# Order of code, branch hints, two moved steps and sums of h in PSUM in an attention, routing and expert kernel

## The chip, the cores and the metric

The kernel runs on one core of a Trainium2 chip. The metric is device time in microseconds (us) of one execution. The core has five engines that run their own instruction streams and meet through semaphores: TensorE (PE, matrix products into PSUM; its weight loads are listed as PEld), VectorE (DVE), ScalarE (ACT), GpSimd (POOL) and SyncE (SP, which here issues most DMAs). A suffix q (PEq, ACTq) marks what an engine's sequencer does: branches, semaphores, register work, DMA issues. The granted clock is the share of full speed that the throttle gave TensorE.

## The reference

Three stages: attention with a window and sink tokens, routing of every token to one of 8 experts, and the expert's two-layer network.

```python
B, H, S, D = 4, 8, 768, 64          # n_sink 4, window 128 (inputs)
scores = matmul(q, k.T) / sqrt(D)
keep = (pos_k < n_sink) | ((0 <= rel) & (rel < window))
x = matmul(softmax(where(keep, scores, -1e9)), v)      # -> [B, S, 512]
...
logits = x @ w_gate                  # 8 experts
local = sigmoid(x @ w_local)
e = argmax(logits) if s == 0 or local < 0.5 else the expert of token s - 1
p = softmax(logits)
out = p[e] * (relu(x @ w1[e]) @ w2[e])     # w1: 512 x 1024, w2: 1024 x 512
```

All inputs are fp32. The kernel gets the products' accuracy by splitting a number into a high part (rounded to fp32r) and a low part (the rest): x w = xh wh + xl wh + xh wl. So each matrix has a "high" tile, made by a cast, and a "low" tile, made by a subtraction.

## The kernel before

**Attention, twice.** `attention(fast)` is traced twice under one runtime `If` (L985): once for a narrow window with few sinks (`narrow != 0`, what these inputs take), once as the general code (`Else`). Both are instructions in one program, the fast code in front and the general code behind it. All five engines meet the branch at the start; at the end of the fast code they branch over the general code to the join, where the rest of the program begins.

**Early expert steps.** While the fast attention runs out, the first expert's first 256 tokens ("early") go through the first layer. There are FC = 8 steps f, one for each 128 of the 1024 hidden columns. `early_first(f, hs)` (its matmuls are L449, its activation L453, its subtraction L454) makes one: 12 matmuls into the PSUM tile `hs`, relu on ScalarE for the high part, and on VectorE max(h, 0) minus the high part for the low part. The matmuls and the activation are issued at the call; the subtraction is the function it returns, called later (`low_steps`). In the fast code the order of TensorE, ScalarE, VectorE and SP is written out by hand, so each engine runs its instructions as the code lists them. The tail of that list is `first_steps(5)`, `low_steps(2)`, `first_steps(6, 7)`, `low_steps(4)`.

**Behind the join** (L1232 on, also in an order by hand): SP issues three loads of weights; ScalarE casts the second layer's weights w2 of the first expert to their high part in 8 instructions (`second_high`, L1226), VectorE makes the low parts in 8 subtractions; then TensorE multiplies the early tokens' relu(h) with w2 high (`late_product`, L1229, 32 matmuls). SP fetches the next rows of x from DRAM, where the attention and the routing have scattered them (`xrsn`, L1054), TensorE transposes them (L425), and the products with w2 low follow. ScalarE, VectorE and POOL also prepare the weights of the coming expert: a cast (L1028) and a subtraction (L1029, part of them on POOL).

**Experts.** For each of the 8 experts a `Switch` chooses one of 25 arms by the number of token groups left. Its dispatch branches stand in the profile at L1421, its hints at L1264 and, as the first instruction of an arm, L1295. In an arm, `ffn1` runs the first layer over a group of ng units of 32 tokens (n = 32 ng columns), again in 8 steps f. For ng <= MERGE = 7 a step accumulates two halves side by side into one PSUM tile `hp` of [128, 2, n] (L1111), VectorE adds the two halves (L1114, a reduction) into an SBUF tile `hs`, ScalarE takes relu of `hs` (L1131) and VectorE the low part (`low`, L1099, which reads `hs` and the high part in `hq`). For larger groups the PSUM tile itself is `hs` (L1120). `ps_h` has three buffers. Between the steps, transposes of the next rows of x (L425) with a cast (L428), a subtraction (L431) and copies of metadata (L427) are put in, and after them come the second layer's products (L1169), the scaling by the gate (L1150) and the scatter to the output (L1151, a DMA issued by POOL).

Of the kernel before, what the change touches and what calls it, by code (L numbers as in the profile page):

```python
# [9 lines left out]
F32 = mybir.dt.float32  # L10
# [7 lines left out]
ET = mybir.EngineType  # L18

P = 128  # L20
HT = 32
# [7 lines left out]
KC = DM // P  # L29
FC = FF // P  # L30
# [12 lines left out]
NE = 2  # L43
MERGE = 7
LIMIT = 24
WARM = 12
STEPS = {2: 1, 3: 2, 4: 1, 5: 1, 9: 1, 10: 1, 11: 2}
ENDING = {38: 1, 39: 2, 40: 1, 41: 1, 42: 1, 43: 1, 44: 2, 45: 1, 46: 2}
# [20 lines left out]
def kernel(ctx, tc, qkd, vn, vs, w1, w2, nw, c_misc, c_ident, c_idw, c_small,  # L69
# [3 lines left out]

    const = ctx.enter_context(tc.tile_pool(name="const", bufs=1))
    dram = ctx.enter_context(tc.tile_pool(name="dram", bufs=1, space=bass.MemoryType.DRAM))

    x_a = const.tile([P, KC * 2 * GMAX * P], F32R, name="x_a")
    xm_a = [const.tile([P, GMAX + 1, 2], I32, name=f"xm{t}") for t in range(2)]
# [136 lines left out]
    with tc.issue_after(flag_op.ins) if FLAGF else ExitStack():  # L215
        for f in lead0[0:2]:
            f()

    narrow = nc.values_load(flag_i[0:1, 0:1], min_val=0, max_val=1,
                            skip_runtime_bounds_check_because="a product of comparisons")  # L220
# [222 lines left out]
    n_e = NE * P  # L443
# [67 lines left out]
    def attention(fast):  # L511
        sfx = "f" if fast else "g"
        with ExitStack() as st:
# [227 lines left out]
            if fast:  # L741
# [62 lines left out]
                for n in range(nb):  # L804
                    now, a, z, y = (blocks[x] if 0 <= x < nb else [] for x in (n, n - 1, n - 2, n - 3))
                    nm = f"{sfx}{n}"
# [54 lines left out]
                nm = f"{sfx}{nb}"  # L861
# [12 lines left out]
                def first_steps(*fs):  # L874
                    for f in fs:
                        if f in (4, 5):
                            pl, tag, w = ((ps_a, "a", n_e), (ps_b, "b", 512))[f - 4]
                            hs = pl.tile([P, w], F32, tag=tag, name=f"he{sfx}{f}")[:, 0:n_e]
                        else:
                            if f % 2 == 0:  # L880
                                first_ps.append(ps_s.tile([P, 2, 512], F32, tag="s", name=f"he{sfx}{f}"))
                            hs = first_ps[-1][:, f % 2, 0:n_e]
                        lows_f.append(early_first(f, hs))
# [3 lines left out]
                def low_steps(k):  # L887
                    for _ in range(k):
                        lows_f.pop(0)()
# [53 lines left out]
                next(tail_r, None)  # L943
                masked()
                first_steps(5)
                low_steps(2)
                first_steps(6, 7)
                low_steps(4)
                order.close()
            else:  # L950
# [28 lines left out]
                    low()  # L979
                counts(ps_m, m_tag)  # L980
                masked()
                for f in range(FC):
                    early_first(f, ps_s.tile([P, 2, 512], F32, tag="s", name=f"he{sfx}{f}")[:, 0, 0:n_e])()

    with tc.If(narrow != 0) as branch:  # L985
        attention(True)
    with branch.Else():
        attention(False)
# [6 lines left out]
    s_p = ctx.enter_context(tc.tile_pool(name="sp", bufs=2))  # L995
    ps_h = ctx.enter_context(tc.tile_pool(name="ps_h", bufs=3, space=PS))
# [12 lines left out]
    def w_load(i, behind=None):  # L1009
        e, c = divmod(i, NCH)  # L1010
        if e >= E:
            return
        t = raw_t[i % AHEAD]
        if c < KC:
            d = nc.sync.dma_start(t, w1[e, c * P:(c + 1) * P, :])
            if behind is not None:
                tc.add_manual_dep(d.ins, behind.ins.name, mybir.DependencyInfo(
                    mybir.DependencyClass.Sync, mybir.DependencyReason.DATA), reason="behind the jumps")
        else:
            w2_load(t, e, c - KC)  # L1020
# [70 lines left out]
    def ffn1(e, xt, ng, nm, ag):  # L1091
        xx, meta = xt
        h1, l1 = w1_of(e)
        n = ng * HT
        held = []

        def low(cuts):
            for d, h in cuts:
                nc.vector.scalar_tensor_tensor(out=d[:, :, 1, :], in0=h, scalar=0.0,  # L1099
                                               in1=d.bitcast(F32)[:, :, 0, :], op0=ALU.max, op1=ALU.subtract)  # L1100

        for f in range(FC):
            fs = slice(f * P, (f + 1) * P)
            if ng <= MERGE:
                hp = ps_h.tile([P, 2, n], F32, tag="h", name=f"h{nm}_{f}")
                m = 2 if ng <= 4 else 1
                mm = [x for k in range(KC) for x in ((hp, h1[:, k, fs], xx[:, k, :, :n]),
                                                     (hp[:, 0:m, :], l1[:, k, fs], xx[:, k, 0:m, :n]))]
                mm[-2:] = mm[:-3:-1]
                for t, (o, w, x) in enumerate(mm):  # L1110
                    nc.tensor.matmul(o, w, x, start=t == 0, stop=t == len(mm) - 1, skip_group_check=True)  # L1111
                hs = s_p.tile([P, MERGE * HT], F32, tag="hs", name=f"hs{nm}_{f}")
                hs = hs[:, :n]
                nc.vector.tensor_reduce(out=hs, in_=hp.rearrange("p a n -> p n a"), axis=AX.X, op=ALU.add)  # L1114
            else:
                hs = ps_h.tile([P, GMAX * P], F32, tag="h", name=f"h{nm}_{f}")
                hs = hs[:, :n]
                mm = [(w, xx[:, k, a, :n], k) for k in range(KC) for w, a in ((h1, 0), (h1, 1), (l1, 0))]
                for t, (w, x, k) in enumerate(mm):
                    nc.tensor.matmul(hs, w[:, k, fs], x, start=t == 0, stop=t == len(mm) - 1)  # L1120
            rest, nf = n % P, n // P * P
            cuts = []
            if rest:
                r = hx[:, f, 2 * nf:2 * nf + 2 * (rest if nf else P)]
                cuts.append((r.rearrange("p (j a c) -> p j a c", j=1, a=2)[:, :, :, 0:rest],
                             hs[:, nf:n].rearrange("p (j c) -> p j c", j=1)))
            if nf:
                cuts.append((hx[:, f, 0:2 * nf].rearrange("p (j a c) -> p j a c", a=2, c=P),
                             hs[:, 0:nf].rearrange("p (j c) -> p j c", c=P)))
            for d, h in cuts:  # L1130
                relu = nc.scalar.activation(d[:, :, 0, :], h, AF.Relu)  # L1131
            if f == 0:
                ag.begun = relu
            if ng > MERGE:
                low(cuts)
            else:
                low(held)
                held = cuts
            ag.run(time1(ng) / FC)
        low(held)  # L1140
# [81 lines left out]
    h2, l2 = w2_of(0)  # L1222

    def second_high(raw, h):
        for s in halves:
            nc.scalar.copy(h[:, s], raw[:, s])  # L1226
# [5 lines left out]
    with tc.manual_schedule(engines=set(ORDERED)):  # L1232
        for c in range(3):
            w_load(NCH + c)
        for c in range(KC):
            h, l = h2(2 * c, 2), l2(2 * c, 2)
            second_high(second_raw[c], h)
            for s in halves:
                last_low = nc.vector.tensor_tensor(out=l[:, s], in0=second_raw[c][:, s], in1=h.bitcast(F32)[:, s],
                                                   op=ALU.subtract)  # L1240
        for f in range(FC):
            for j in (1, 0):
                for a in range(2):
                    late_product(f, j, a, h2, start=f + a == 0)
# [21 lines left out]
    for c in range(2):  # L1266
        h, l = [t[:, c, :] for t in w1_of(1)]
# [157 lines left out]
```

## Time and profile before

| | us |
|---|---|
| median of 3 runs | 578.47 |
| lowest, highest run | 575.3, 579.16 |
| the profiled execution, device time | 580.11 |
| its span, first to last instruction | 578.3 |
| TensorE busy | 526.2 (91%) |
| mean granted clock | 0.954 |

The profile shows one execution. Busy times are sums of the instructions' times on an engine; matmuls are pipelined, so their ends are modelled. A timeline lists an engine's instructions in order of start, with equal neighbours put together (x24 is 24 of them) and in brackets the idle time before them and the instruction that ended it. A line of a group gives the shortest, median and longest duration in ns, the first and last start in us, and the shapes. A row of a window gives its length, then each engine's busy time, the granted clock, the share of time in which the DMA engines were busy, and GB/s.

In 40 equal slices of 14.5 us the busy tenths of TensorE, and the granted clock, are:

```profile
PE   6699989979997989787999999899999799999994
PEclk8599989899998989989899999999999899999999
```

### The profile page before, as it was taken

What the parts mean: (1) busy time and instruction counts of PE and PEld (TensorE: products, weight loads), DVE (VectorE), ACT (ScalarE), POOL (GpSimd) and SP (SyncE); (2) the same over time, 40 slices, a digit from 0 to 9 for tenths busy, and PEclk for the clock granted to TensorE, in tenths of its full rate; (3) what the DMA queues carried; (4) which work ended last, traced back from release to release, by engine and by line L of the source; (5) the groups of instructions that cost most, each with busy time, mean ns of one, the idle gap of its engine ahead of it and who ended that gap; (6) DMA issues with size and microseconds to landing.
All of it is one profiled execution on the core that took longest, in us unless ns stands there. A gap on an engine that the chain in (4) does not pass through costs nothing. (4 is left out here: it accounts for less than half of the span.)

```text
span 578.3 us, 11794 instructions
## 1 busy us (share of the span) xinstructions
PE 526.2 (91%) x3933; PEld 451.0 (78%) x3933; DVE 343.4 (59%) x1270; ACT 285.0 (49%) x854; POOL 228.2 (39%) x191
## 2 busy tenths in 40 slices
PE   6699989979997989787999999899999799999994
PEld 3588878868886879676889697889888489889893
DVE  4587777687777777647256274653474937363321
ACT  3588868667766785253253080633432635024120
POOL 3963625475265073334260062443502635204101
PEclk8599989899998989989899999999999899999999
DMA  8624404170436025374571274747514656111000
GB/s 300 234 117 177 155 22 176 38 238 32 154 112 201 2 111 183 132 224 141 184 247 39 78 272 112 262 134 239 205 40 141 239 170 245 55 30 50 19 23 35
DMA packets 30474, 80.53 MB, mean 139 GB/s; under 512 B 3646, under 2 KB 5310, under 8 KB 30272
## 3 DMA queue, kind: packets, MB, share of 16 engines
q1 hardware_dynamic: 25520, 65.41, 33.3%
q0 software_dynamic: 4176, 12.64, 5.8%
q14 instruction: 148, 1.21, 0.7%
q8 instruction: 54, 0.88, 0.6%
q10 hardware_dynamic: 576, 0.39, 0.2%
HBM read 63.41 MB, written 16.06 MB: 137 GB/s over the span
## 5 line engine op out<-in xcount | busy, mean ns | idle before, releaser
L619 ACT ACTIVATE pef<-smf,biasf 128x264 f32<-128x264 f32 (+2 forms) x192 | 93.6, 489 | 42.9 <-DVE biasf L616 42.7
L1131 ACT ACTIVATE hq<-h 128x256 fp32r<-128x256 f32 (+3 forms) x72 | 24.2, 360 | 110.4 <-PE h L1120 94.7
L616 DVE CUSTOM_DVE_ANT_0 smf<-sf,mask 128x264 f32<-128x264 f32 (+2 forms) x192 | 66.6, 402 | 10.3 <-PE sf L604 9.7
L1169 PE MATMUL late<-w_a,hq 128*128 128x512 f32 (+2 forms) x288 | 70.2, 398 | 1.2 <-issue 1.2
L1099 DVE SCALAR_TENSOR_TENSOR hq<-h,hq 128x256 fp32r<-128x256 f32 (+3 forms) x72 | 26.6, 390 | 68.6 <-ACT hq L1131 67.1
L1169 PEld LDWEIGHTS late<-w_a,hq 128*128 128x128 f32 (+2 forms) x288 | 50.8, 179 | 15.8 <-issue 1.7
L1151 POOL DMA_INDIRECT out_dram<-ot_d,oi_d x18 | 18.7, 1036 | 94.0 <-DVE ot_d L1150 74.3
L634 PE MATMUL tpf<-ident,pef 128*128 128x128 f32 x352 | 55.2, 302 | 0.2
L641 ACT COPY ptf<-tpf 128x512 f32<-128x512 f32 (+1 forms) x96 | 50.9, 531 | 1.6 <-PE tpf L634 1.6
L1131 ACT ACTIVATE hq<-hs 128x96 fp32r<-128x96 f32 (+2 forms) x72 | 16.7, 273 | 68.2 <-DVE hs L1114 61.0
L670 PE MATMUL avf<-ptf,v 128*64 128x128 f32 x704 | 50.2, 284 | 0.0
L634 PEld LDWEIGHTS tpf<-ident,pef 128*128 128x128 f32 x352 | 41.8, 152 | 7.8 <-issue 1.1
L1169 PE MATMUL late<-w_b,hq 128*128 128x512 f32 (+1 forms) x168 | 42.1, 409 | 0.8 <-ACT x_a L428 0.8
L670 PEld LDWEIGHTS avf<-ptf,v 128*64 128x64 f32 x704 | 38.5, 139 | 4.9 <-issue 0.3
L576 DVE TENSOR_TENSOR xb<-bkf,rsf 128x256 f32<-128x256 f32 x48 | 20.3, 423 | 32.8 <-ACT ptsf L651 31.2
L1169 PEld LDWEIGHTS late<-w_b,hq 128*128 128x128 f32 (+1 forms) x168 | 32.0, 192 | 9.5 <-ACT x_a L428 1.2
L1029 POOL TENSOR_TENSOR w_c<-raw,w_c 128x1024 fp32r<-128x1024 f32 x10 | 25.1, 2515 | 33.5 <-ACT w_c L1028 22.8
L1029 POOL TENSOR_TENSOR w_a<-raw,w_a 128x1024 fp32r<-128x1024 f32 x10 | 26.5, 2652 | 27.7 <-ACT w_a L1028 25.5
L604 PE MATMUL sf<-w_a 64*128 64x264 f32 (+2 forms) x288 | 28.2, 330 | 9.3 <-POOL w_a L134 6.5
L619 ACT ACTIVATION_READ_ACCUMULATOR pef<-smf,biasf 128x1 f32 x192 | 36.3, 189 | 0.0
L560 PE MATMUL bkf<-idw,xtf 128*128 128x146 f32 x192 | 34.7, 306 | 0.4
L1120 PEld LDWEIGHTS h<-x_a,w_c 128*128 128x128 f32 x288 | 34.3, 188 | 0.7 <-issue 0.6
(218 smaller groups left out, 1116.1 us busy)
## 6 DMA issues: line engine op xcount, KB each, us to landing
raw<-in_dram SPq DMA_DIRECT2D x53, 512.0 KB, 5.4
raw<-in_dram SPq DMA_DIRECT2D x14, 800.0 KB, 5.8
xr_0n<-xs SPq DMA_DIRECT2D x21, 258.0 KB, 4.2
v<-in_dram SPq DMA_DIRECT2D x7, 768.0 KB, 4.3
raw_w<-in_dram SPq DMA_DIRECT2D x7, 512.0 KB, 5.6
raw<-in_dram SPq DMA_DIRECT2D x10, 256.0 KB, 4.7
xs<-zrow SPq DMA_DIRECT2D x9, 258.0 KB, 5.5
xr_0r<-xs SPq DMA_DIRECT2D x8, 258.0 KB, 3.3
```

The lines of the kernel that those rows point to most:

```text
L560: mm = nc.tensor.matmul(bk[:, pr * WX:(pr + 1) * WX], blk["xt"][:, pr, :], idw[:, g * NPR + pr, :], start=True, stop=True, skip_group_chec ...
L604: u["mm"] = nc.tensor.matmul(sps[:, t, :w], qx[ROWS[t], i * P:(i + 1) * P], kx[ROWS[t], off:off + w], start=m == 0, stop=m == 2)
L616: u["dve"] = nc.vector.tensor_tensor_reduce(out=sm[:, :w], in0=sps[:, t, :w], in1=mk, scale=-0.125, scalar=BIG, op0=ALU.add, op1=ALU.min, ...
L619: nc.scalar.activation(pe[:, h, :w], sm[:, :w], AF.Exp, bias=bias[:, t:t + 1], scale=-1.0, accum_out=z[:, h, 0:1])
L634: nc.tensor.transpose(tp[:, t, k, :], pe[:, 2 * c + t, o:o + P], ident)
L641: nc.scalar.copy(pt[:, :, 0:nt, :], tp[:, :, 0:nt, :])
L670: nc.tensor.matmul(avt[ROWS[t], pr, :], prep["v"][:, j, 2 * pr + t, :], x["pt"][:, t, k, :], start=i < 2 and pr == 0 and k == 0, stop=pr = ...
L1029: todo += [lambda s=s: lo(out=l[:, s], in0=raw[:, s], in1=h.bitcast(F32)[:, s], op=ALU.subtract) for s in ([slice(0, FF)] if eng[1] == "po ...
L1099: nc.vector.scalar_tensor_tensor(out=d[:, :, 1, :], in0=h, scalar=0.0, in1=d.bitcast(F32)[:, :, 0, :], op0=ALU.max, op1=ALU.subtract)
L1120: nc.tensor.matmul(hs, w[:, k, fs], x, start=t == 0, stop=t == len(mm) - 1)
L1131: relu = nc.scalar.activation(d[:, :, 0, :], h, AF.Relu)
L1169: nc.tensor.matmul(o, a, w, start=t == 0, stop=t == len(mm) - 1, skip_group_check=half)
```

## The change

1. **Order of code.** `If` gets a label and `preferred_fallthrough_block=False`: the general code now stands in front and the fast code behind it. At the start every engine that takes the fast code branches over the general code; at the end of the fast code it goes on into the join without a jump. A hint with the branch's target ("LikelyTaken") is issued by each of the five engines as the first instruction of the kernel.
2. **Early steps.** `FIRST_F = 6`: the attention makes steps 0 to 5 only. Steps 6 and 7 move behind the join, into the block written out by hand, each with a PSUM tile of its own from `ps_h`. On ScalarE the order becomes: two casts of w2, the activation of step 6, two casts, the activation of step 7, four casts. On VectorE the two subtractions of steps 6 and 7 come first, then the eight of w2's low part.
3. **Sums of h.** Where 3n <= 512, that is for ng <= 5, the PSUM tile gets a third part of n columns, and the reduction writes the sum `hs` there and not into SBUF. The activation and the low part then read it from PSUM.

```diff
@@ -43,6 +43,7 @@
 NE = 2
 MERGE = 7
 LIMIT = 24
+FIRST_F = 6
 WARM = 12
 STEPS = {2: 1, 3: 2, 4: 1, 5: 1, 9: 1, 10: 1, 11: 2}
 ENDING = {38: 1, 39: 2, 40: 1, 41: 1, 42: 1, 43: 1, 44: 2, 45: 1, 46: 2}
@@ -73,6 +74,8 @@
 
     const = ctx.enter_context(tc.tile_pool(name="const", bufs=1))
     dram = ctx.enter_context(tc.tile_pool(name="dram", bufs=1, space=bass.MemoryType.DRAM))
+
+    tc.mark_branch_hint_location("mode", "LikelyTaken", engines=[ET.SP, ET.DVE, ET.PE, ET.Activation, ET.Pool])
 
     x_a = const.tile([P, KC * 2 * GMAX * P], F32R, name="x_a")
     xm_a = [const.tile([P, GMAX + 1, 2], I32, name=f"xm{t}") for t in range(2)]
@@ -943,8 +946,6 @@
                 next(tail_r, None)
                 masked()
                 first_steps(5)
-                low_steps(2)
-                first_steps(6, 7)
                 low_steps(4)
                 order.close()
             else:
@@ -979,10 +980,10 @@
                     low()
                 counts(ps_m, m_tag)
                 masked()
-                for f in range(FC):
+                for f in range(FIRST_F):
                     early_first(f, ps_s.tile([P, 2, 512], F32, tag="s", name=f"he{sfx}{f}")[:, 0, 0:n_e])()
 
-    with tc.If(narrow != 0) as branch:
+    with tc.If(narrow != 0, preferred_fallthrough_block=False, label="mode") as branch:
         attention(True)
     with branch.Else():
         attention(False)
@@ -1102,15 +1103,18 @@
         for f in range(FC):
             fs = slice(f * P, (f + 1) * P)
             if ng <= MERGE:
-                hp = ps_h.tile([P, 2, n], F32, tag="h", name=f"h{nm}_{f}")
+                hp3 = ps_h.tile([P, 3 if 3 * n <= 512 else 2, n], F32, tag="h", name=f"h{nm}_{f}")
+                hp = hp3[:, 0:2]
                 m = 2 if ng <= 4 else 1
                 mm = [x for k in range(KC) for x in ((hp, h1[:, k, fs], xx[:, k, :, :n]),
                                                      (hp[:, 0:m, :], l1[:, k, fs], xx[:, k, 0:m, :n]))]
                 mm[-2:] = mm[:-3:-1]
                 for t, (o, w, x) in enumerate(mm):
                     nc.tensor.matmul(o, w, x, start=t == 0, stop=t == len(mm) - 1, skip_group_check=True)
-                hs = s_p.tile([P, MERGE * HT], F32, tag="hs", name=f"hs{nm}_{f}")
-                hs = hs[:, :n]
+                if 3 * n <= 512:
+                    hs = hp3[:, 2]
+                else:
+                    hs = s_p.tile([P, MERGE * HT], F32, tag="hs", name=f"hs{nm}_{f}")[:, :n]
                 nc.vector.tensor_reduce(out=hs, in_=hp.rearrange("p a n -> p n a"), axis=AX.X, op=ALU.add)
             else:
                 hs = ps_h.tile([P, GMAX * P], F32, tag="h", name=f"h{nm}_{f}")
@@ -1232,9 +1236,18 @@
     with tc.manual_schedule(engines=set(ORDERED)):
         for c in range(3):
             w_load(NCH + c)
+        first_lows = []
         for c in range(KC):
             h, l = h2(2 * c, 2), l2(2 * c, 2)
             second_high(second_raw[c], h)
+            if FIRST_F + c < FC:
+                first_lows.append(early_first(FIRST_F + c, ps_h.tile([P, n_e], F32, tag="h", name=f"hl{c}")))
+            elif first_lows:
+                for f in first_lows:
+                    f()
+                first_lows = []
+        for c in range(KC):
+            h, l = h2(2 * c, 2), l2(2 * c, 2)
             for s in halves:
                 last_low = nc.vector.tensor_tensor(out=l[:, s], in0=second_raw[c][:, s], in1=h.bitcast(F32)[:, s],
                                                    op=ALU.subtract)
```

## The prediction

> **What bounds the kernel now.** I read the page first, then TensorE's timeline from the end of the attention on, then the windows of granted clock, and then, at every stop of TensorE, the timelines of the engine that it waited for.
>
> ```profile
> span 578.3 us, 11794 instructions
> PE 526.2 (91%) x3933; PEld 451.0 (78%) x3933; DVE 343.4 (59%) x1270; ACT 285.0 (49%) x854; POOL 228.2 (39%) x191
> ```
>
> TensorE is busy for 91% of the span. So time is won only where TensorE stands still or runs slowly, and work taken off another engine counts only if TensorE waits for it. The profiled execution took 580.11 us, 1.81 more than its span and 1.64 above the median of 578.47; I add my sum to the median. Its timeline (start, time taken, what; in brackets the idle time before it and who ended it):
>
> ```profile
> 237.90 3.04 PE L449 MATMUL hef<-x_a,w_a 128*128 128x256 f32 x24
> 241.42 1.68 PE L449 MATMUL hef<-x_a,w_a 128*128 128x256 f32 x12 [0.47 <-ACT hq L453]
> 247.40 9.26 PE L1229 MATMUL late<-w_b,hq 128*128 128x512 f32 x32 [4.30 <-ACT w_b L1226]
> 256.50 1.03 PE L425 MATMUL xpsn<-ident,xrsn 128*128 128x128 f32 x8
> 261.57 2.79 PE L1111 MATMUL h<-x_b,w_a 128*128 128x128 f32 x24
> 269.51 0.62 PE L425 MATMUL xp_0n<-ident,xr_0n 128*128 128x128 f32 x4
> 273.54 1.09 PE L425 MATMUL xp_0n<-ident,xr_0n 128*128 128x128 f32 x4 [3.41 <-issue]
> 275.47 7.49 PE L1169 MATMUL late<-w_b,hq 128*128 128x512 f32 x24 [0.84 <-ACT x_a L428]
> 453.88 1.09 PE L425 MATMUL xp_0n<-ident,xr_0n 128*128 128x128 f32 x4 [2.76 <-issue]
> ```
>
> Three stops stand out: 4.30 us where the attention ends (the join), 3.41 us in the first expert, 2.76 us in the sixth. Behind each the clock falls. In the windows (length, busy time of PE, PEld, DVE, ACT, POOL, granted clock) that follow a window with over 2 us of idle TensorE, it is 0.50:
>
> ```profile
> 244.97:248.39 3.42, 0.99 (x4) 0.86 (x5) 0.85 (x2) 1.73 (x4) 0.00 (x0) 1.00 0.33 90
> 248.39:251.80 3.41, 3.41 (x9) 2.65 (x8) 2.09 (x4) 3.41 (x7) 0.00 (x0) 0.50 0.82 216
> 251.80:255.20 3.40, 3.40 (x16) 2.73 (x15) 2.30 (x8) 1.20 (x3) 1.12 (x1) 1.00 0.87 262
> 272.28:275.70 3.42, 1.32 (x5) 0.98 (x6) 3.15 (x13) 1.31 (x3) 1.48 (x2) 0.50 0.37 103
> 275.70:279.11 3.41, 3.41 (x9) 2.64 (x10) 0.27 (x1) 0.00 (x0) 0.00 (x0) 0.50 0.89 286
> 453.19:456.60 3.41, 2.71 (x9) 1.70 (x10) 3.41 (x11) 3.41 (x10) 0.62 (x1) 0.50 0.88 326
> ```
>
> At 0.50 some 8 products of 512 columns begin in 3.41 us (0.427 us each), at full clock between 14 and 15 (0.235). A slow window full of work costs about 1.5 us.
>
> **The join, part by part.** The fast attention ends with the two last early steps (6 and 7); then the engines jump over the general attention's code.
>
> ```profile
> L985 PEldq COMPARE_BRANCH  x2: 83/2012/3942, 5.8 to 241.5; - x2
> 243.14 0.38 ACT L453 ACTIVATE hq<-hef 128x256 fp32r<-128x256 f32 x1 [1.77 <-PE hef L449]
> 246.66 4.26 ACT L1226 CAST w_b<-raw 128x512 fp32r<-128x512 f32 x8 [3.14 <-PEq L1258]
> 239.61 1.41 DVE L454 SCALAR_TENSOR_TENSOR hq<-hef,hq 128x256 fp32r<-128x256 f32 x4
> 246.31 1.86 SPq L1054 DMA_DIRECT2D xrsn<-xs  x3
> ```
>
> TensorE's branch at 241.5 takes 3.94 us against 0.08 at the kernel's start, where it falls through; ScalarE, done at 243.52, casts again at 246.66 (3.14 idle). Both are late by the same jump, so both must lose it, and with the fast code behind the general code both do. Removed: 4.30 idle, the 0.47 wait between steps 6 and 7 (one shared tile before, two now), and the slow window 1.5: 6.3 us.
>
> What is late next: TensorE may have to wait behind the join for the other engines' last work in the attention. Nothing before shows that wait. Its nearest row is VectorE's four sums for steps 2 to 5, which end at 241.02. Step 5 ends at about 239.42 (half of the 3.04 us for 24 matmuls from 237.90), so up to 1.6 us come back. Bounds: no wait, and one until 246.3, when SP fetches rows of x (behind the last scatter), which puts the products about where they stand. I take the 1.6: **4.7 us won** (0 to 6.3). The moved work itself (24 matmuls, 2 activations at 0.38, 2 of VectorE's sums) counts the same in both places, and issues no DMA. On ScalarE the activations now stand among the eight casts (4.26 us for all); a pair of casts takes 1.1 us while TensorE has 3.0 us of steps, so this is covered; without that cover TensorE would wait one pair, 1.1 us. VectorE's subtractions on w2 now follow the two sums, with all casts ahead of them. The rows of x are asked for at 246.31 to 248.17 and land 3.2 us later, by 251.4; TensorE, with 241.0 + 3.0 of steps + 32 products at 0.235, reaches them at 251.6. So they are just in time, and winning more than 4.9 us here would meet this load.
>
> ```profile
> xrsn<-xs SPq DMA_DIRECT2D x3, 258.0 KB, 3.2
> ```
>
> **The sums of h in PSUM.** The condition 3n <= 512 holds up to n = 160: by the reductions below (8 steps f a group) for three groups, one of 64 columns (first expert) and two of 160 (fifth, sixth).
>
> ```profile
> L1114 DVE TENSOR_REDUCE hs<-h x40: 275/492/626, 264.2 to 513.5; 128x224 f32<-128x448 f32 x16, 128x160 f32<-128x320 f32 x16, 128x64 f32<-128x128 f32 x8
> 268.09 4.66 POOL L1029 TENSOR_TENSOR w_c<-raw,w_c 128x1024 fp32r<-128x1024 f32 x2 [4.88 <-DMA raw_w<-in_dram]
> 268.34 2.20 DVE L1099 SCALAR_TENSOR_TENSOR hq<-hs,hq 128x64 fp32r<-128x64 f32 x1
> 270.85 1.99 DVE L1099 SCALAR_TENSOR_TENSOR hq<-hs,hq 128x64 fp32r<-128x64 f32 x1
> 272.76 0.68 DVE L431 TENSOR_TENSOR x_a<-xp_0n,x_a 128x512 fp32r<-128x512 f32 x1
> 449.67 2.37 POOL L1029 TENSOR_TENSOR w_c<-raw,w_c 128x1024 fp32r<-128x1024 f32 x1 [1.30 <-PE h L1111]
> 449.71 2.57 DVE L1099 SCALAR_TENSOR_TENSOR hq<-hs,hq 128x32 fp32r<-128x32 f32 x2
> L1099 DVE SCALAR_TENSOR_TENSOR hq<-hs,hq x72: 176/263/2373, 264.9 to 515.2; 128x128 fp32r<-128x128 f32 x32, 128x96 fp32r<-128x96 f32 x16, 128x32 fp32r<-128x32 f32 x16, 128x64 fp32r<-128x64 f32 x8
> L1099 DVE SCALAR_TENSOR_TENSOR hq<-h,hq x72: 179/418/557, 285.1 to 560.2; 128x256 fp32r<-128x256 f32 x48, 128x32 fp32r<-128x32 f32 x8, 128x96 fp32r<-128x96 f32 x8, 128x384 fp32r<-128x384 f32 x8
> ```
>
> The low part of relu(h) (L1099) reads hs and hq. With hs in SBUF it takes 0.18 us at best and up to 2.37: each long one lies under a POOL subtraction (L1029) and ends with it (268.34 + 2.20 = 270.54; POOL's first half ends at about 270.4). The same form that reads its first input from PSUM (hq<-h) never exceeds 0.56, for shapes up to twelve times as wide, and starts from the same 0.18 (for 32 columns): so I take the lock away and no change of the free duration. The trace has no reduction that writes PSUM; as its input is in PSUM already I put it at no change, 0 +/- 0.5 for the 24 steps (an estimate: 20 ns a step either way).
>
> First expert: TensorE stood for 3.41 us until VectorE, locked twice, came to L431 (272.76 to 273.44); two slow windows follow, with 1.32 and 3.41 us of matmuls at half speed, some 2.3 us lost. Removed 5.7.
>
> Sixth: 2.76 idle to 453.88, again behind a lock (2.57 us at 449.71), and 2.71 us at half speed, 1.2 lost (part of that window is idle). Removed 4.0. The fifth has no such stop.
>
> What is late next: a buffer of h comes free when hs has been read for the last time, by L1099, and no longer when the sum has been taken. There are three; step f+3 of TensorE needs the low part of f, which stands behind the sum of f+1 and behind ScalarE's activation, and that behind casts:
>
> ```profile
> 264.61 0.26 ACT L1131 ACTIVATE hq<-hs 128x64 fp32r<-128x64 f32 x1 [4.13 <-DVE hs L1114]
> 264.78 1.12 ACT L1028 CAST w_c<-raw 128x512 fp32r<-128x512 f32 x2
> 265.81 0.25 ACT L1131 ACTIVATE hq<-hs 128x64 fp32r<-128x64 f32 x1
> ```
>
> TensorE makes a step in 0.93 us (24 matmuls, three steps, in 2.79); ScalarE, with two casts (1.12 together) between the activations at 264.61 and 265.81, in 1.20. Over four steps with casts this runs 4 times 0.27, 1.1 us, behind. I charge it in the first and the sixth expert, and 0.4 in the fifth, whose pace I estimate as less tight. Residual stops, since the transposes wait for loads and VectorE's L431 anyway: 0.5 in the first, 0.9 in the sixth. **First expert: 5.7 - 1.1 - 0.5 = 4.1 won** (bounds -1.1, where only the later release acts, to 5.7); **sixth: 4.0 - 1.1 - 0.9 = 2.0** (-1.1 to 4.0); **fifth: -0.4** (0 to -1.0).
>
> **The order of code and the hints.** The general code now stands in front, so the jump that the join loses moves to the start, where all five engines go over it to the fast code. Instructions of hints themselves cost 0.05 us each. What would hide a late engine there:
>
> ```profile
> 14.78 1.62 POOL L129 CAST hq<-raw 128x800 fp32r<-128x800 f32 x2 [0.82 <-DMA raw<-in_dram]
> 21.52 0.81 PE L604 MATMUL sf<-w_a 64*128 64x264 f32 x4 [2.55 <-POOL w_a L134]
> L1264 ACTq BRANCH_PREFETCH_HINT  x1: 50/50/50, 247.5 to 247.5; - x1
> L1421 ACTq COMPARE_BRANCH  x16: 37/42/63, 260.1 to 559.9; - x16
> L1295 ACTq BRANCH_PREFETCH_HINT  x8: 36/40/40, 262.6 to 520.7; - x8
> ```
>
> TensorE waits 2.55 us for POOL at 21.52, and POOL for a load at 14.78. A jump of 3 us on TensorE, VectorE or ScalarE right behind its branch, TensorE's being at 5.8, lies ahead of these waits; only one on SP, which still has loads to ask for, delays them in full. Nearest rows for a jump with a hint: ScalarE's at the dispatch, hinted at 247.5, branches at 260.1 and begins its arm at 262.6, 2.5 us later. So: 0 (hidden, or the hint holds) to 2.5 (SP unhinted in effect). I take **-0.3**, since the hints are the first instructions, 5.8 us ahead of TensorE's branch (the L985 row), and all engines but SP have cover.
>
> [...]
>
> **Sum.** Join 4.7 + first expert 4.1 + sixth 2.0 - fifth 0.4 - start 0.3 = 10.1 us. The profiled execution would take 570.0, the median **568.4**.
>
> **The rivals.**
>
> *The PSUM sums win nothing.* POOL's subtraction then holds up VectorE's next operation with two inputs in SBUF (its own share of L1029), or the later release eats the gain. For it: TensorE waits for L431, not for L1099. Against it: 2.20 and 1.99 us are each an L1099. What is left is 4.7 - 0.4 - 0.3 = 4.0: 574.5.
>
> *The start pays the jump.* The hints come to nothing, as ScalarE's at the dispatch; SP's loads come 2.5 us late and TensorE's wait of 21.52 with them. 568.4 + 2.2 = 570.6. Against it: TensorE's wait is for POOL, which has slack to its own load only at 14.78.
>
> *The join stays* (the change doesn't do what it says): the engines still fetch there, now the shared code, or TensorE is held until the scatter at 246.3. Join 0: 578.47 - 5.4 = 573.1. For it: the 3.94 us don't tell a jump from another fetch. Against it: the first L985 branch on TensorE, which falls through, takes 0.083.
>
> *Slower: h runs out of buffers.* Place: steps 3 to 7 of the three groups, 15 in all, where TensorE needs a buffer back. Each that waits for a whole further step of ScalarE and VectorE costs about one step of TensorE, 1.0 us. Beside the 4.0 of join, fifth and start it turns slower than before from the fifth lost step on, if the locks win nothing; with 8 lost it gives 578.5 - 4.0 + 8 = 582.5. For it: ScalarE's 1.20 exceeds 0.93. Against it: three buffers give two steps of slack.
>
> [...]
>
> **How the numbers follow.** Forecast 0.52, PSUM wins nothing 0.18, start pays 0.12, join stays 0.11, out of buffers 0.07. A change within 1% (5.8 us) is about what a measurement of this kernel can't tell from none: the edge is 572.7. Faster: 0.50 of the forecast, 0.10 of the start, 0.05 and 0.02 of the other two, 0.67. Slower: 0.05 of the buffers. Same: the rest, 0.28. The range begins where every gain is whole (6.3 + 5.7 + 4.0 = 16.0, 562.5) and ends at 576.5, 2.0 beyond the rival at 574.5 (the start's other 2.2); it leaves out the last rival and the edges.
>
> **What would show it.** Join: TensorE's branch (L985) at some 240 takes 0.1, not 3.94; ScalarE's 3.14 idle is gone, and no window at 0.50 follows; wrong if h2's products (L1229) begin after 246. Sums: no L1099 above 0.6 in the three groups, no idle over 1 us at the transposes after 268 and 450; wrong if TensorE's matmuls of h (L1111) have idle of more than 1 us a group, ended by VectorE's L1099. Start: L604's last wait ends by 22; wrong if SP's loads after 7 us come 2 us later.

## The result, and the profile after

The changed kernel takes 581.22 us (median of 20 runs, 578.9 to 586.55), the kernel before 578.32 (20 runs beside them, 572.47 to 588.23). The ratio is 1.0074, 95% interval 1.005 to 1.0099: some 3 to 4 us slower, where 10 us faster was forecast. The ratios here and below are taken from the fast runs alone (those within 1.5% of the fastest of their kernel), so they need not equal the quotient of two medians, here 1.0050. The profiled execution of the changed kernel took 579.70 us, 1.5 below its median; that of before, 580.11, lay 1.8 above the median of the 20 runs. The two profiles, 0.4 us apart, thus hide the 2.9 us between the medians, and the reading goes by stages, not by the two spans.

First the changed kernel's page, then TensorE's timeline at the start (L604 is now L607, L1111 L1113, L1099 L1100):

```profile
PE 525.0 (91%) x3933; PEld 449.6 (78%) x3933; DVE 338.1 (59%) x1270; ACT 283.3 (49%) x854; POOL 227.5 (39%) x191
15.79 0.47 PE L607 MATMUL sf<-w_a 64*128 64x128 f32 x2 [8.35 <-DVE w_a L132]
25.03 1.14 PE L607 MATMUL sf<-w_a 64*128 64x264 f32 x4 [0.66 <-POOL w_a L137]
```

The batch that began at 21.52 begins at 25.03, 3.5 us later, after TensorE has waited 8.35 us for VectorE at 15.79. ScalarE's and VectorE's timelines, the branch's rows and a window (DMA share and GB/s are its last two columns) say why; the last row is VectorE's same cast in the kernel before:

```profile
11.15 0.40 ACT L132 CAST w_a<-raw 128x256 fp32r<-128x256 f32 x1 [5.57 <-issue]
15.35 0.29 DVE L132 CAST w_a<-raw 128x256 fp32r<-128x256 f32 x1 [6.68 <-issue]
L986 PEldq COMPARE_BRANCH  x1: 489/489/489, 6.2 to 6.2; - x1
L986 DVEq COMPARE_BRANCH  x1: 78/78/78, 8.8 to 8.8; - x1
8.00:10.00 2.00, 0.00 (x0) 0.00 (x0) 0.64 (x3) 0.00 (x0) 0.00 (x0) 0.66 1.03 368
8.54 0.29 DVE L129 CAST w_a<-raw 128x256 fp32r<-128x256 f32 x1 [0.32 <-DVE mask L211]
```

Both engines branch and then do nothing for 5.6 and 6.7 us that the profile lays to no semaphore ("issue"): the jump. TensorE's took only 0.49. Meanwhile the DMA engines are full (share 1.03). From 6.2 to 15.3 us the queues that the page lists as "instruction" moved 6 packets, the only sign here of a fetch; in the kernel before, whose branch falls through at this place, they moved none from 5.8 to 15.3, and 3 during the jump at its join (241.5 to 245.4). The jump that cost 3 to 4 us at the join costs nearly twice that here, and VectorE has work due.

TensorE's timeline at the join, and ScalarE's:

```profile
243.32 3.04 PE L452 MATMUL hl<-x_a,w_a 128*128 128x256 f32 x24 [1.29 <-DVE hq L457]
246.21 3.91 PE L1233 MATMUL late<-w_b,hq 128*128 128x512 f32 x16
252.28 1.22 PE L428 MATMUL xpsn<-ident,xrsn 128*128 128x128 f32 x8 [2.16 <-DMA xrsn<-xs]
253.25 6.08 PE L1233 MATMUL late<-w_b,hq 128*128 128x512 f32 x24
245.33 1.13 ACT L1230 CAST w_b<-raw 128x512 fp32r<-128x512 f32 x2
249.39 2.18 ACT L1230 CAST w_c<-raw 128x512 fp32r<-128x512 f32 x4 [2.92 <-DMA xs<-xb,slotf]
251.47 0.37 ACT L456 ACTIVATE hq<-hl 128x256 fp32r<-128x256 f32 x1
251.75 2.17 ACT L1230 CAST w_b<-raw 128x512 fp32r<-128x512 f32 x4
```

The stop of 4.30 is gone, a wait of 1.29 for VectorE's sums in its place. But the engines no longer run the block as the code lists it. ScalarE does the four casts for the *next* expert (w_c) ahead of step 7's activation and of w2's last four casts, and stands 2.92 us until the scatters have read the memory where w_c will lie. TensorE has the transposes of x in the middle of the products and stands 2.16 us for their load. The scheduler had merged the two blocks behind the join, though each keeps its own order.

The first expert, on TensorE, ScalarE and VectorE (rows, windows and the group of all L1100 with hs in PSUM):

```profile
267.04 4.79 PE L1113 MATMUL h<-x_b,w_a 128*128 128x128 f32 x24 [2.44 <-DVE hq L1100]
266.41 0.22 ACT L1135 ACTIVATE hq<-h 128x64 fp32r<-128x64 f32 x1 [5.69 <-issue]
262.92 0.30 DVE L1118 TENSOR_REDUCE h<-h 128x64 f32<-128x128 f32 x1 [0.76 <-PE h L1113]
268.80:272.20 3.40, 3.40 (x18) 3.40 (x18) 1.14 (x6) 0.58 (x4) 3.40 (x2) 0.50 0.90 275
L1100 DVE SCALAR_TENSOR_TENSOR hq<-h,hq x112: 173/344/558, 266.7 to 559.8; 128x256 fp32r<-128x256 f32 x48, 128x32 fp32r<-128x32 f32 x24, 128x128 fp32r<-128x128 f32 x16, 128x64 fp32r<-128x64 f32 x8
```

VectorE's lock is gone, as forecast: none of the L1100 that read PSUM takes over 0.56 us. But VectorE has the first sum done at 263.2, and TensorE goes on only at 267.04: the buffer is free when L1100 has read it, L1100 needs ScalarE's activation, and ScalarE arrives 5.69 us after its last work, from the jump into the arm. Then the clock is halved (0.50 from 268.8 to 272.2).

In the fifth and the sixth expert, TensorE's rows (the first is the fifth's; the last is the like of the third in the kernel before):

```profile
437.42 5.85 PE L1173 MATMUL late<-w_a,hq 128*128 128x512 f32 x24 [0.42 <-issue]
454.69 0.60 PE L428 MATMUL xp_0n<-ident,xr_0n 128*128 128x128 f32 x4
460.95 5.83 PE L1173 MATMUL late<-w_c,hq 128*128 128x512 f32 x24 [1.05 <-issue]
460.73 5.83 PE L1169 MATMUL late<-w_c,hq 128*128 128x512 f32 x24 [0.33 <-issue]
```

The stop of 2.76 us ahead of the sixth's transposes is gone. Ahead of the next products TensorE stands 1.05 us where it stood 0.33, and 0.42 in the fifth, where it had no stop.

By stages, from the start of the same matmul in two traces (us against the profile of before; "attention" is the stretch from the fourth batch of L604 to step 5, "join" from step 5 to the first product with w2, "to arm" from there to the first h of the first arm, "first layer" from there to that arm's first L1169, "rest" from there to the first h with the next expert's weights, "fifth" and "sixth" from the first h of a group of 160 columns to the first h of what follows it):

```
kernel         start  attention  join  to arm  first layer  rest  fifth  sixth
after          +3.5     -1.0     -3.7   +1.4     +1.7      -0.2   +1.1   -2.8
after_again    +3.3     +0.4     -3.7   +1.2     +2.4      -0.2   +1.3   -2.7
order_only     +3.5    +10.2     -1.9    0.0     -1.1      +1.9   -0.1   +0.3
sums_only      +0.1     +4.7     +1.2   +0.5     +0.6      -0.1   +2.2   -1.9
sums160        -0.1     -0.6      0.0   +1.0     +0.1      -0.7   +1.5   -2.4
no_hints       +2.4     +9.5     -3.7   +0.3     +2.8      +0.6   +1.7   -2.4
one_block      +3.3     +5.4     -3.7   -1.6     +3.7      +1.0   +1.4   -2.6
mend1          +3.1     -2.9     -3.7   -1.6     +2.4      +0.4   +1.4   -2.1
mend2          +3.2    +10.4     -3.7   -1.6     -1.0      +0.4   +1.2   -2.9
mend4           0.0    +10.1     -1.1   -1.6     +1.4      +0.7   +1.8   -2.6
mend5          +3.4     +1.8     -3.7   -1.6     -0.7      +0.7   +1.3   -2.6
loads_later    +0.1     +7.2     +1.1   +0.6     +2.9      +0.1   +1.2   -2.4
```

The attention has no edit, and it moves by up to 10 us between chips and executions (the kernel before itself had medians from 578.3 to 590.9 in the sets beside these runs). So each ratio below is to the kernel before in the same set. Each row is one profile, and a stage whose code is unchanged moves too (the join by 1.2 us in `sums_only`), so a sum over stages is good to some 2 us. The two groups of 160 columns moved alike wherever hs lies in PSUM: the fifth expert's first layer +0.7, the sixth's +1.0, and the sixth's stop with the slow clock behind it -4.2, of which a longer stop ahead of the next products took 0.6 to 0.7 back. As wholes the fifth lost 1.1 to 2.2 us and the sixth won 1.9 to 2.9.

### The profile page after: what moved, and what is told of

Read it like the earlier page. It is cut to its first block, busy times and chain, and to the rows that moved or that the text cites. A ratio compares the mean times of both kernels' runs of the same rounds, so it can differ in the third digit from the quotient of the medians.

```text
span 577.9 us, 11823 instructions
## 1 busy us (share of the span) xinstructions
PE 525.0 (91%) x3933; PEld 449.6 (78%) x3933; DVE 338.1 (59%) x1270; ACT 283.3 (49%) x854; POOL 227.5 (39%) x191
## 5 line engine op out<-in xcount | busy, mean ns | idle before, releaser
L1135 ACT ACTIVATE hq<-h 128x32 fp32r<-128x32 f32 (+4 forms) x112 | 31.9, 316 | 145.8 <-PE h L1124 93.0
L1100 DVE SCALAR_TENSOR_TENSOR hq<-h,hq 128x32 fp32r<-128x32 f32 (+4 forms) x112 | 34.5, 331 | 73.1 <-ACT hq L1135 67.0
L1173 PE MATMUL late<-w_b,hq 128*128 128x512 f32 (+1 forms) x168 | 40.9, 400 | 0.0
L607 PE MATMUL sf<-w_a 64*128 64x264 f32 (+2 forms) x288 | 28.0, 327 | 12.8 <-DVE w_a L132 8.3
L607 PEld LDWEIGHTS sf<-w_a 64*128 64x128 f32 x288 | 21.6, 207 | 18.6 <-issue 13.2
L1124 PE MATMUL h<-x_a,w_c 128*128 128x256 f32 x288 | 34.6, 281 | 0.8 <-PE late L1173 0.8
L1030 POOL TENSOR_TENSOR w_a<-raw,w_a 128x1024 fp32r<-128x1024 f32 x10 | 24.6, 2462 | 26.4 <-ACT w_a L1029 24.3
```

Of the source, the lines that this page charges most:

```text
L607: u["mm"] = nc.tensor.matmul(sps[:, t, :w], qx[ROWS[t], i * P:(i + 1) * P], kx[ROWS[t], off:off + w], start=m == 0, stop=m == 2)
L1030: todo += [lambda s=s: lo(out=l[:, s], in0=raw[:, s], in1=h.bitcast(F32)[:, s], op=ALU.subtract) for s in ([slice(0, FF)] if eng[1] == "po ...
L1173: nc.tensor.matmul(o, a, w, start=t == 0, stop=t == len(mm) - 1, skip_group_check=half)
```

## The experiments

**Each part alone.** `order_only` is the kernel before with the new order of code and the hints; `sums_only` has only hs in PSUM; `no_hints` is the changed kernel without this line:

```diff
-    tc.mark_branch_hint_location("mode", "LikelyTaken", engines=[ET.SP, ET.DVE, ET.PE, ET.Activation, ET.Pool])
```

> The kernel before with part 1 alone (general code in front, hints). Theory (the jump is only moved): ScalarE and VectorE stand 5 to 7 us behind their branch at the start, as in the changed kernel, and TensorE's products of L604 come 3 to 4 us late there; the 4.3 us stop and the slow window at the join go. Net -1 to -2.5 us: 576 to 577.5. Rival (the start's delay is caused by something else in the change, or is absorbed later): 572 to 574.

Ratio 0.9982 (0.9943 to 1.002). The start is late by 3.5 us as in the changed kernel, and at the join TensorE's row shows what stands in place of the jump:

```profile
259.21 3.15 PE L1231 MATMUL late<-w_b,hq 128*128 128x512 f32 x8 [2.19 <-DVE hq L456]
```

It waits 2.19 us for step 7's sums, and the products still run slowly (8 in 3.15 us, 0.39 each, against 0.235 at full clock in the kernel before). So the order of code alone wins 1.9 us at the join, the moved steps alone win 1.1 (`mend4` below), and both together 3.7. The ratio can't tell the theory from no change. The stages bear out its start (stops of 6.20 us on ScalarE and 6.84 on VectorE), but not its join, where the whole stop with its slow window was to go.

> The changed kernel without its five hints. Theory (the hints come too early or are lost for ScalarE and VectorE): their stops at the start stay at 5 to 7 us, TensorE's branch rises from 0.49 to 3 us or more, but TensorE waits for VectorE anyway: within 1 us of the changed kernel, 580.5 to 582. Rival (the hints help, or their own fetches add to the crowd): over 2 us slower, or over 1 us faster.

Ratio 0.9987 (0.9956 to 1.0018). TensorE's branch, and VectorE's first row behind its own:

```profile
L984 PEldq COMPARE_BRANCH  x1: 6004/6004/6004, 5.5 to 5.5; - x1
14.31 0.29 DVE L130 CAST w_a<-raw 128x256 fp32r<-128x256 f32 x1 [6.35 <-DMA v<-in_dram]
```

(The load named there only landed last; the cast doesn't read v.) The hint saves TensorE 5.5 us (0.49 against 6.00), which it then spends waiting for VectorE. VectorE's stop is 6.35 without and 6.68 with a hint, ScalarE's 5.99 and 5.57. For these two engines the hints did nothing that shows, and the start is 1.1 us earlier without any. The ratios of this set and of the changed kernel come from different chips. By them the kernel without hints would be the faster by 3.6 to 5 us; its stages (1.8 us lost, against 1.0 and 1.6 in the two profiles of the changed kernel, the attention left out) don't show that, so whether the hints cost time in all stays open.

> The kernel before with part 3 alone (hs in PSUM for ng <= 5). Theory A (the later release of h hurts only because ScalarE came late into the first arm of the changed kernel): with ScalarE in its arm as early as before, first expert -2 to -4 us, fifth +1, sixth -3: 572 to 575. Theory B (three buffers are too few by themselves): TensorE waits over 2 us for VectorE's L1099 in the first expert and runs at clock 0.50 again, first expert +1, fifth +1, sixth -3: 577 to 578.

Ratio 0.997 (0.9935 to 1.0005). The first layers of the fifth and the sixth came as expected, the two experts as wholes less well (+2.2 and -1.9). The first expert lies between the theories: the lock is gone, TensorE waits only 0.78 us, and the clock falls all the same. The TensorE row, the window that holds the wait, and the next one:

```profile
271.55 5.36 PE L1112 MATMUL h<-x_b,w_a 128*128 128x128 f32 x24 [0.78 <-DVE hq L1099]
268.00:271.40 3.40, 2.77 (x25) 2.63 (x23) 1.06 (x5) 0.48 (x2) 1.01 (x1) 1.00 0.85 247
271.40:274.80 3.40, 3.25 (x16) 3.28 (x16) 1.57 (x7) 2.27 (x7) 0.55 (x1) 0.51 0.51 198
```

A window with 2.77 us of work in 3.40 is followed by half speed: 24 matmuls in 5.36 instead of 2.79 us.

**Is a jump longer when the DMA engines are full?** `load_at_join` is the kernel before with a copy of 2 MB that nothing reads:

```diff
     pad(0)
+    spare = dram.tile([KC * P, FF], F32, name="spare")
+    nc.sync.dma_start(spare, w1[0])
```

> The kernel before with one copy of 2 MB from DRAM to DRAM, issued by SP just before the join (it changes no output). Theory (a jump's fetch takes longer when the DMA engines are full, which is why it takes 5 to 7 us at the start): TensorE's branch at the join rises from 3.9 us to 5 to 7, ScalarE's stop from 3.1 to over 5, with a DMA share near 1. Rival (the start's jump is long for another reason, such as five engines fetching at once): both stay within 0.5 us of 3.9 and 3.1.

582.83 us in its one run. TensorE's branch (the second of its two), the window that it fills, and ScalarE's row behind its own branch; then the window that TensorE's branch fills in the kernel before:

```profile
L985 PEldq COMPARE_BRANCH  x2: 83/3750/7417, 5.7 to 239.8; - x2
239.80:247.20 7.40, 1.64 (x12) 1.44 (x12) 0.76 (x2) 0.39 (x1) 1.54 (x2) 0.92 1.08 344
250.69 4.26 ACT L1226 CAST w_b<-raw 128x512 fp32r<-128x512 f32 x8 [8.82 <-DMA spare<-in_dram]
```

```profile
241.50:245.40 3.90, 1.60 (x12) 1.40 (x12) 0.76 (x2) 0.38 (x1) 1.52 (x2) 1.00 0.70 253
```

7.42 us at a DMA share of 1.08, where it was 3.94 at 0.70. The same jump at the same place takes 3.5 us longer under load. ScalarE's stop grows from 3.14 to 8.82 us; the profile names the landing of the copy as its end, though nothing reads the copy.

**The changed kernel again**, as a measure on the chip of `mend1` and `sums160`:

> The changed kernel once more, as the measure for the others of this chip: stops at the start, join and first arm as in its first profile (TensorE's fourth batch of L604 3 to 4 us late, first arm with a wait of over 2 us for VectorE's L1100); time against before between -0.2% and +1%.

581.82 us, ratio 1.005 (1.0018 to 1.0083), with the stops of the first profile: the fourth batch of L604 3.3 us late, and 2.60 us of waiting for L1100 in the first arm.

**The order behind the join.** `one_block` opens the second block's schedule at the first:

```diff
-    with tc.manual_schedule(engines=set(ORDERED)):
-        for c in range(3):
+    ctx.enter_context(tc.manual_schedule(engines=set(ORDERED)))
+    if True:
+        for c in range(3):
...
-    ctx.enter_context(tc.manual_schedule(engines=set(ORDERED)))
```

> The changed kernel with the two blocks behind the join made into one, so that each engine keeps the order of the code there. Theory (the moved steps made the scheduler put ScalarE's casts for the next expert ahead of the activation of step 7 and of the last four casts of w2, and TensorE's transposes of x ahead of the second half of the products): ScalarE's stop of 2.9 us and TensorE's of 2.2 us go, the first arm begins 1.5 to 2.5 us earlier relative to the attention's end: 578.5 to 580 against 581.2. Rival (the rows of x decide when the arm begins, in whatever order): no change, 581.

Ratio 0.9976 (0.994 to 1.0011). The arm begins 3.0 us sooner after the first product than in the changed kernel (-1.6 against +1.4). Then it gives 2.0 us of that back in the first layer and 1.2 behind it, so at the end of the first expert nothing is left of it. TensorE's and VectorE's rows:

```profile
271.61 5.36 PE L1113 MATMUL h<-x_b,w_a 128*128 128x128 f32 x24 [3.85 <-DVE hq L1100]
270.59 0.50 DVE L1118 TENSOR_REDUCE h<-h 128x64 f32<-128x128 f32 x2 [5.26 <-issue]
```

TensorE is in the arm early, VectorE 5.26 us after its last work: the next jump has become the limit.

**The sums in the wider groups alone.** `sums160` is the kernel before with hs in PSUM where 4 <= ng <= 5; `mend1` is `one_block` with the same condition.

> The kernel before with the sums in PSUM for the groups of 4 and 5 units only, that is the two of 160 columns. First expert unchanged; fifth +0.5 to +1.2 us; sixth -1.5 to -3: 0.5 to 2 us faster than before. Rival (what is won in the sixth is lost in a later wait): no change at the end.

Ratio 0.9974 (0.9943 to 1.0004): of the size expected, not certain.

> The changed kernel with one block behind the join and the sums in PSUM only for the groups of 4 and 5 units. Theory (in the first expert the sums in PSUM make TensorE wait for ScalarE, which comes late into the arm, where before it waited for VectorE alone): from the first h of the arm to its late products as before or up to 1 us more, where one_block had 3.65 us more; time 3 to 6 us under the changed kernel and 1 to 4 us under the kernel before. Rival (TensorE waits for the late engines either way, and VectorE's locked L1099 cost as much): the stretch as in one_block, time within 1 us of it.

Ratio 0.998 (0.9946 to 1.0013). The time is where the theory put it: 576.93 us, against 581.82 for the changed kernel on the same chip. The stretch (the first layer) came to +2.4, neither theory's value. The timelines of VectorE and TensorE:

```profile
261.51 0.49 DVE L1118 TENSOR_REDUCE hs<-h 128x64 f32<-128x128 f32 x2 [4.65 <-issue]
261.85 5.38 PE L1113 MATMUL h<-x_b,w_a 128*128 128x128 f32 x24 [2.56 <-DVE hs L1118]
```

With hs in SBUF TensorE waits for VectorE itself, 4.65 us in the jump. So the later release of h is not the cause alone: whichever engine must free the buffer comes late, and frees it later still if it needs ScalarE too (TensorE waits 2.56 us here, 3.85 in `one_block`).

**The loads behind the jump.** What fills the DMA engines there are mostly SP's loads of the second expert's weights: in the changed kernel the DMA share is 0.90 from 260.5 to 266.4 us, and 0.76 is the queue that carries these loads. `mend2` is `mend1` with three of them moved; `mend4` is `mend2` with the fast code in front and no hints; `loads_later` is `sums160` with the same loads moved; `mend5` is `mend2` with the condition of the change, 3n <= 512.

```diff
-    for c in range(3, NCH - 1):
-        w_load(NCH + c)
+    w_load(NCH + 3)
...
                     if not e:
-                        ag.add(0.0, lambda: w_load(2 * NCH - 1))
+                        for c in range(KC, NCH):
+                            ag.add(0.0, lambda c=c: w_load(NCH + c, ag.begun))
```

The second argument of `w_load` holds a load back until the arm's first activation, but the function uses it for loads of w1 only. These are loads of w2, so they wait for no activation: SP issues them when it reaches their place in its own order.

> mend1 with the three loads of the second expert's w2 (512 KB each) issued in the first arm behind its first activation, and not ahead of the jump into it. Theory (the jump of VectorE and ScalarE into the first arm takes 4.6 and 6.5 us in mend1 because these loads fill the DMA engines): both drop to 2 to 4 us, TensorE's wait of 2.56 us after three steps goes, the stretch from first h to late products is 2 to 4 us shorter than in mend1; 573 to 575.5 against 578.8 before. Rival (the jump takes what it takes): no change against mend1, 577.

Ratio 0.9931 (0.9899 to 0.9963): 0.7% faster than before, with the interval clear of 1. VectorE's and TensorE's rows:

```profile
272.18 0.49 DVE L1118 TENSOR_REDUCE hs<-h 128x64 f32<-128x128 f32 x2 [1.96 <-PE h L1113]
269.86 5.56 PE L1113 MATMUL h<-x_b,w_a 128*128 128x128 f32 x48
275.76 2.01 DVE L1100 SCALAR_TENSOR_TENSOR hq<-hs,hq 128x64 fp32r<-128x64 f32 x1
281.30 1.08 PE L428 MATMUL xp_0n<-ident,xr_0n 128*128 128x128 f32 x4 [3.22 <-issue]
```

VectorE's idle time falls from 4.65 to 1.96 us, and TensorE runs six steps without a stop, the stretch 3.4 us shorter than in `mend1`. Then comes the old lock (2.01) and the old stop (3.22).

> mend2 without part 1: fast code in front, so no jump at the start and one at the join, with steps 6 and 7 behind it. Theory (the start's jump costs 3.1 to 3.5 us and the join's 3.7 to 5 with its slow window, so part 1 is worth 0 to 1.5 us once the rest is mended): mend4 0 to 1.5 us slower than mend2. Rival (the join's jump is worth all of the 6.3 us priced): mend4 3 us or more slower.

Ratio 0.9927 (0.9895 to 0.9958), the same as `mend2`. The order of code with its hints is worth nothing that can be measured: 3.2 us are lost at the start and 2.6 won at the join; the first layer, 2.5 us shorter in `mend2`, doesn't show in the time, with intervals of 0.3% either way.

> sums160 (fast code in front, steps 6 and 7 in the attention) with the same three loads issued behind the jump into the first arm. Theory: the engines' jump into the arm shortens here as well, but TensorE is late itself by the join's jump, so 0 to 1.5 us won against sums160: 575.5 to 577 against 578.8 before. Rival (loads that come later are missed later): slower than sums160.

Ratio 1.0029 (0.9994 to 1.0064), where `sums160` had 0.9974 on another chip: the side of the rival, though the intervals meet. The rows of SP, VectorE and TensorE say why the first layer took 2.9 us more than before:

```profile
264.54 1.42 SPq L492 DMA_DIRECT2D raw<-in_dram  x3
276.01 0.49 DVE L1117 TENSOR_REDUCE hs<-h 128x64 f32<-128x128 f32 x2 [5.12 <-issue]
276.36 5.38 PE L1112 MATMUL h<-x_b,w_a 128*128 128x128 f32 x24 [3.03 <-DVE hs L1117]
```

SP is in the arm early here and issues the three loads 6.0 us ahead of the arm's first matmul (270.53), so they fall into VectorE's jump, whose stop is 5.12 us where `sums160` has 2.79. The same order holds in all the profiles. With the first of these loads 9 to 12 us ahead of the arm's first matmul (the kernel before 10.1, `sums160`, `sums_only`, `order_only`, `load_at_join`) TensorE waits 0.8 us at most for a buffer in the first layer. With it 4.9 to 6.0 us ahead (the changed kernel 4.9, `after_again`, `no_hints`, `one_block`, `mend1`, `loads_later`) it waits 2.4 to 3.9 us. In `mend4`, 1.5 ahead, it waits 1.68; in `mend5` and `mend2`, 1.2 and 1.4 behind it, 0.62 and not at all.

> mend2 with the sums in PSUM for all three groups again, that is the changed kernel with one block and the three loads behind the jump into the first arm. Theory A (the later release of h cost 1.7 to 2.4 us in the first expert only because ScalarE and VectorE came late into the arm): they come 2 to 4 us after their last work, no L1100 takes over 0.6 us, TensorE waits under 0.7 us and keeps its clock; the stretch from first h to late products is 3 to 5 us shorter than before (mend2: 1.0), ratio to before 0.985 to 0.991. Theory B (three buffers are too few as ScalarE works at 1.2 us a step): TensorE waits 0.7 us or more for L1100 and its clock is halved as in sums_only; the stretch 0 to 2 us longer than before, ratio 0.995 to 1.0.

Ratio 0.9931 (0.99 to 0.9962), as `mend2`. Between the theories again. TensorE's row and two windows:

```profile
264.81 4.25 PE L1113 MATMUL h<-x_b,w_a 128*128 128x128 f32 x24 [0.62 <-DVE hq L1100]
264.30:267.70 3.40, 2.75 (x19) 2.56 (x20) 2.23 (x9) 2.86 (x9) 1.22 (x1) 0.90 0.93 295
267.70:271.10 3.40, 3.40 (x18) 3.40 (x18) 0.54 (x4) 0.81 (x2) 3.40 (x2) 0.50 1.05 333
```

ScalarE is there 3.87 us after its last work, TensorE's wait is down to 0.62, and still the clock halves. So the first expert's sums in PSUM win about what they lose: no lock and no stop of 3.2, but half speed for the last steps. A short stop alone doesn't decide it. Later in the same trace a window with 2.49 us of matmuls and a stop of 0.92 was followed by full clock:

```profile
280.68:284.09 3.41, 2.49 (x18) 2.00 (x17) 0.00 (x0) 0.00 (x0) 0.95 (x1) 1.00 0.73 219
284.09:287.50 3.41, 3.41 (x31) 3.41 (x30) 0.85 (x2) 2.54 (x7) 1.58 (x1) 1.00 0.49 183
```

What tells the two cases apart stays open.

## Why the prediction was wrong

By its own steps, against the stages of the changed kernel's profile:

- **Start, -0.3 forecast, 3.5 lost (3.3 in the second profile).** This is the first step that failed. I priced the jump by ScalarE's at the dispatch (2.5 us) and took 3 us to be covered by the waits for POOL and the loads. The jump took 5.6 to 6.7 us, in the crowd of the first loads (DMA share 1.03); that a full DMA lengthens a jump by such an amount is what `load_at_join` shows (3.94 us at a share of 0.70, 7.42 at 1.08). And the cover that I named (POOL's load at 14.78, TensorE's wait at 21.52) lies behind VectorE's work, which now begins at 15.35: what POOL waits for is late itself. The rival "the start pays the jump" was right in kind, wrong in the engine (SP's loads come 0.5 to 0.7 us late, VectorE's work 6.8) and too cheap at 2.2. VectorE and ScalarE paid the jump (stops of 6.7 and 5.6 us); on TensorE the hint took the wait away (0.49 us with it, 6.00 without).
- **Join, +4.7 forecast.** The mechanism was right: the jump's stop went, and VectorE's sums gave back 1.29 us (1.6 taken). The products came 3.7 us earlier. But 1.4 of it were gone at the arm, where the slow window's end should have added 1.6 (`one_block`). The step that failed is "the activations now stand among the eight casts": it took the order of the code for the order of the engines. From step 5 to the arm the gain was 2.2 us, and 5.3 with the order kept, though that gain was lost again behind the jump into the arm.
- **First expert, +4.1 forecast, 1.4 lost** (first layer +1.68, the rest -0.25). The lock went, as said. What failed is "what is late next": I counted ScalarE's pace inside the arm (1.1 us) and not its arrival. The new release runs through ScalarE, whose jump took 5.69 us under loads that were already on their way (DMA share 0.90 from 260.5 to 266.4): the change itself had brought them from 10.1 to 4.9 us ahead of the arm's first matmul. `mend2` shows it for VectorE, whose idle time falls from 4.65 to 1.96 with the loads behind its jump, and `loads_later` shows the reverse. And a stop under 1 us was followed by half clock (0.78 us, then 0.51, in `sums_only`; 0.62, then 0.50, in `mend5`), so most of the 5.7 us that I removed came back with the engines nearer to time as well (first layer and rest together +0.5 and 0.0). By its own price of a slow window, the 2.3 within that 5.7 should have been 2.1.
- **Sixth, +2.0 forecast, 2.8 won; fifth, -0.4 forecast, 1.1 lost.** Here the working holds for the sixth: 4.0 removed (4.2 measured), 1.1 put back for the later release (1.04 measured), and of the 0.9 for residual stops 0.7 came, ahead of its last products, with 0.4 won back ahead of the seventh. In the fifth 0.7 is the first layer; with the new stop of 0.42 the whole is a little beyond the bound of 1.0.
- **The sum.** 10.1 us was forecast. These stages come to 3.5 - 3.7 + 1.4 + 1.4 + 1.1 - 2.8 = 0.9 us lost, and to 1.6 in the second profile. Where the rest of the 2.9 between the medians goes, the profiles don't show.
- **The rival "h runs out of buffers"** was nearest. TensorE did wait for a buffer of h, once for 2.44 us, until its last reader (L1100) was done, not for many steps.

The range began at the right rivals but held no two of them at once: start, order and first expert all went wrong together, and two of these three (start and first expert) have one cause, a jump priced without its DMA load. Measured were 581.22 us, where the range ended at 576.5.

## What to carry to other kernels

Price a jump by where it lands: here the same jump took 3.9 us at a DMA share of 0.70 and 7.4 at 1.08, so a jump that is moved into a crowd of loads can cost at the new place what it saved at the old (3.5 us lost at the start, 3.7 won at the join). Look at when the loads near a jump are issued, in the trace and not in the code: the same edit brought them behind the jump in `mend2` (0.7% faster than before) and into it in `loads_later` (no faster). When the last reader of a buffer changes, ask when that reader's engine *arrives*, not only how fast it runs. And read the order of each engine from the trace after moving work across a block: here an order written by hand held inside its block only.

## What the runs showed of the hardware

- A hint as the first instruction took TensorE's branch from 6.00 (`no_hints`) to 0.49 us; ScalarE's and VectorE's stops stayed at 5.6 to 6.7.
- A stop of 0.62 to 0.78 us in a window with 2.75 to 2.77 us of matmuls in 3.40 was followed by a granted clock of 0.50 to 0.51 in the next window and at least one more (`sums_only`, `mend5`), but one with 2.49 in 3.41 and a stop of 0.92 was not (`mend5`). I had taken over 2 us of idle for the sign of it.
- VectorE's L1099 or L1100 with one input in PSUM took 0.56 us at most in the profiles of the two kernels; with both inputs in SBUF, those held up took 1.3 to 2.4 us (before, `mend1`, `mend2`).
- TensorE's jump at the join took 3.94 us at a DMA share of 0.70 and 7.42 at 1.08 (`load_at_join`).
